# One K tile's multiply, add and score split into two halves of its keys, in a one-core decode kernel

## The chip, the core and the metric

The kernel runs on one core of a Trainium2 chip. The metric is device time in microseconds (us) of one execution. A core has five engines that run side by side: TensorE (PE; its weight loads are shown as PEld), VectorE (DVE), ScalarE (ACT), GpSimd (POOL) and SyncE (SP). Each works through its own instructions in order and waits on semaphores for the others. Sixteen DMA engines move data between the large memory (HBM) and the core's own memory; here SyncE issues nearly all of these transfers.

## The reference

One token goes through attention over a long cache (32 heads, 65,536 keys of 128 numbers each, bf16) and, beside it, through a small gated feed-forward network; a scalar gate mixes the two.

```python
def _A_ref(x, k_cache, v_cache, wq, wo):
    q = (x @ wq).reshape(B, Sq, H, Dh) -> (B, H, Sq, Dh)
    scores = einsum("bhqd,bhkd->bhqk", q, k_cache) * (Dh ** -0.5)
    p = softmax(scores)
    o = einsum("bhqk,bhkd->bhqd", p, v_cache)
    return o.reshape(B, Sq, H * Dh) @ wo

def _B_ref(x, w_gate, w_up, w_down):
    return (silu(x @ w_gate) * (x @ w_up)) @ w_down

g = sigmoid((x * gate_w).sum(-1))
return g * _A_ref(x, ...) + (1 - g) * _B_ref(x, ...)
```

K and V are 512 MB each, and every byte is read once. There are few operations per byte.

## The kernel before

**Tiles.** A head's 65,536 keys are four tiles of 128 partitions x 128 keys; tile n belongs to head n // 4. Two tiles form a pair m = n // 2, loaded by one 8.4 MB transfer (some are loaded as two tiles). K pairs alternate between two buffers (`K_bufs`), V pairs share one (`V_buf`). With one query, the scores are not made by a matrix product with K: VectorE multiplies a K tile by the query, which is repeated over the keys (`product`, L281), and then adds the upper half of the 128 columns to the lower half (`add_halves`, L293, or `add_once`, L304). TensorE adds up what is left: `scores` (L508) multiplies groups of 4 columns by a unit matrix and accumulates them in PSUM, so that 64 columns take 16 matrix products of 512 columns (128 keys x 4) each. VectorE reduces the last 4 to one score for each key (`fold`, L315). ScalarE makes the exponentials, and TensorE multiplies them with the V tiles (`values`, L531, 64 products for a pair).

**Stages.** A prologue written out by hand does the queries of all heads, the feed-forward network, and the scores of the first head (tiles 0 to 3). Then a loop goes over the pairs: in step m the scores of K pair m and the values of V pair m - 2. The change lies in the prologue.

**Order on the engines in the prologue.** After tile 2's product and addition VectorE runs the gate's operations on the feed-forward network: it waits for ScalarE's exponential `eg`, adds one, takes the reciprocal, and multiplies with the two projections (L636 to L641), which gives `hT`. TensorE uses `hT` in the product with w_down (L643, 14 matrix products, into `b_ps`); ScalarE scales that row, TensorE takes it into the output's accumulators (L651), and spreads the second head's query over the partitions (`query_spread`, L521). VectorE meanwhile multiplies tile 3 (`product(3)`), reduces tile 2, adds tile 3 (`add_halves(3)`), and TensorE makes tile 3's scores (`scores_direct(3)`). `fold(3)` and the maximum over the head's scores (`row_max`, L321) follow, and then the loop begins with tile 4.

**Transfers around the change.** SyncE issues, in its program's order: the third K pair when the scores of tile 1 are done (L629), the first V pair into `V_buf` when w_down's product is done, as w_down lies in that buffer (L654), the fourth K pair when tile 3's scores are done (event `pe_D`, L665), and in the loop the second V pair when the values of the first are done (`load_v`, L201), followed by the next K pair.

**Events.** `dv` counts VectorE's finished instructions, `pe_D` the tiles scored in the prologue, `pe_x` some of TensorE's products. `wait(engine, events, value)` holds that engine until the count is reached.

Of the kernel before, what the change touches and what calls it, by code (L numbers as in the profile page):

```python
# [8 lines left out]
ALU = mybir.AluOpType  # L9
AXIS = mybir.AxisListType  # L10
P = 128
NB = 128
PAIR = 2 * NB
QUAD = 4


WIDE = 64
# [24 lines left out]
def kernel(  # L42
# [18 lines left out]
    _, H, Sk, Dh = A_k_cache.shape  # L61
# [17 lines left out]
    def sb(name, shape, dtype=f32):  # L79
        return consts.tile(shape, dtype, name=name)  # L80
# [3 lines left out]

    K_bufs = [ring.tile([P, PAIR * Dh], bf16, name=f"K{i}_buf") for i in range(2)]
    V_buf = ring.tile([P, PAIR * Dh], bf16, name="V_buf")
# [8 lines left out]
    ident_b, ones_b, q_diag = (sb(n, [P, P], bf16) for n in ("ident_b", "ones_b", "q_diag"))  # L95
# [16 lines left out]
    S_ps = [psum.tile([P, NB, QUAD], f32, name=f"S{i}_ps") for i in range(2)]  # L112
# [14 lines left out]
    def halves(buf):  # L127
        return [buf[:, i * NB * Dh : (i + 1) * NB * Dh].rearrange("p (j d) -> p j d", d=Dh) for i in range(2)]

    K_half, V_half = [halves(b) for b in K_bufs], halves(V_buf)  # L130
# [3 lines left out]
    def v_view(n):  # L134
        return {N - 4: K_half[0][1], N - 3: V_half[0], N - 2: V_half[1], N - 1: K_half[1][1]}[n]

    sync, act, dve, pool, pe = nc.sync, nc.scalar, nc.vector, nc.gpsimd, nc.tensor
# [6 lines left out]
    ac, ac_loop, ac_q, dv, dv_loop, dv_top, dv_max, dv_first, dv_rg, out_a, out_b, pe_D, pe_K, pe_q0 = (  # L144
        Events(nc, n)
        for n in (
            "ac", "ac_loop", "ac_q", "dv", "dv_loop", "dv_top", "dv_max", "dv_first", "dv_rg",
            "out_a", "out_b", "pe_D", "pe_K", "pe_q0",
        )
    )  # L150
# [17 lines left out]
    def wait(engine, events, value):  # L168
        key = id(engine), id(events)
        value -= taken.get(key, 0)  # L170
        if seen.get(key, 0) < value:
            engine.wait_ge(events.sem, value)
            seen[key] = value
# [85 lines left out]
    marks = {}  # L259

    own = [dv]

    def product(n):
        K = K_half[n // 2 % 2][n % 2]
        q = q_sb[n // G % 2]
        q_rep = bass.AP(tensor=q.tensor, offset=q[:, :].offset, ap=[list(q[:, :].ap[0]), [0, NB], [1, Dh]])
        m = n // 2

        if m == 0:
            wait(dve, (ka_in, kb_in)[n], 16)  # L270
        elif m == 1:
            wait(dve, kc_in, 16)
        elif n == N - 1:
            wait(dve, kb_in, 32)
        else:
            wait(dve, k_in[m % 2], 16 * (m // 2))
        if n < G:
            wait(dve, ac, marks["q"])
        else:
            wait(dve, ac_q, n // G)  # L280
        return own[0](dve.tensor_tensor(out=K, in0=K, in1=q_rep, op=ALU.mult))  # L281

    def add_halves(n, width, last, out=None, ahead=None):
        K = K_half[n // 2 % 2][n % 2]
        half, mark = Dh // 2, last
        while half >= width:
            wait(dve, own[0], mark)
            to = K[:, :, 0:half]
            if half == width and ahead is not None:
                fold(ahead)  # L290
            if half == width and out is not None:
                to = out
            ins = dve.tensor_tensor(out=to, in0=K[:, :, 0:half], in1=K[:, :, half : 2 * half], op=ALU.add)  # L293
            if half == width and out is not None:
                ins.then_inc(c_S[n % 2], 1)
            else:
                mark = own[0](ins)
            half //= 2
        marks["K", n] = mark

    def add_once(n, last):
        wait(dve, own[0], last)
        K, half = K_half[n // 2 % 2][n % 2], Dh // 2
        dve.tensor_tensor(  # L304
            out=K[:, :, 0:half], in0=K[:, :, 0:half], in1=K[:, :, half:], op=ALU.add
        ).then_inc(c_S[0], 1)


    def fold(n):
        h, g = divmod(n, G)  # L310
        if n < G or n >= N - G:
            wait(dve, pe_D, n + 1 if n < G else n + 1 - N + 2 * G)
        else:
            wait(dve, pe_S, n + 1 - G)
        return own[0](dve.tensor_reduce(  # L315
            out=S_sb[h % 2][:, g * NB : (g + 1) * NB], in_=S_ps[n % 2], axis=AXIS.X, op=ALU.add
        ))
# [19 lines left out]
    def vector_step(m):  # L337
        h, b = divmod(m, MH)
        width, to = (WIDTH, T_sb) if m < M - 2 else (WIDE, None)
        last = product(2 * m)  # L340
        if to is not None:
            add_once(2 * m, last)
        if b == 0:
            top_of(h - 1)
        else:
            fold(2 * m - 1)
        if to is None:
            add_halves(2 * m, width, last)
        last = product(2 * m + 1)
        if b == 1:  # L350
            weight(h - 1, m - 1)
        add_halves(2 * m + 1, width, last, to, 2 * m)
        if b == 1:
            row_max(h, fold(2 * m + 1))
# [31 lines left out]
    def copy(out, in_, scale=1.0):  # L386
        return act.activation(out=out, in_=in_, func=ACT.Copy, scale=scale)  # L387
# [115 lines left out]
        pe.wait_ge(credit, 1)  # L503
        pe.sem_inc(credit, -1)  # L504

    def scores(n, src, width, events):
        for c in range(0, width, QUAD):
            ins = pe.matmul(  # L508
                S_ps[n % 2], lhsT=ident_b, rhs=src[:, :, c : c + QUAD],
                start=(c == 0), stop=(c == width - QUAD),  # L510
            )
            if c == 0 and events is pe_S and n == 1:
                pe_K(ins)
        events(ins)

    def scores_direct(n):
        wait(pe, dv, marks["K", n])
        scores(n, K_half[n // 2 % 2][n % 2], WIDE, pe_D)

    def query_spread(events):  # L520
        events(pe.matmul(qb, lhsT=ones_b, rhs=q_diag, start=True, stop=True))  # L521
# [34 lines left out]
    def prologue():  # L556
        with nc.allow_non_contiguous_dma(reason="small"):
# [3 lines left out]
            out=V_buf[:, : KT * H * Dh], in_=A_wq.rearrange("(p t) f -> p (t f)", t=KT)  # L561
# [17 lines left out]
        for h in range(H):  # L579
            for t in range(KT):  # L580
                ins = pe.matmul(
                    q_all[:, h : h + 1], lhsT=wq_sb[:, t, h * Dh : (h + 1) * Dh],
                    rhs=xT[:, t : t + 1], start=(t == 0), stop=(t == KT - 1),
                )
# [8 lines left out]
        marks["q"] = ac(copy(q_sb[0], qb))  # L593

        add_halves(0, WIDE, product(0))
        scores_direct(0)
        wait(dve, x_in, 16)
        wait(dve, gw_in, 16)
# [6 lines left out]
        last = product(1)  # L605
        fold(0)
        add_halves(1, WIDE, last)
        scores_direct(1)
        wait(dve, ac, marks["eg2"])
        wait(dve, dv, dv(dve.tensor_scalar_add(eg2, eg2, 1.0)))  # L610
        wait(dve, dv, dv(dve.reciprocal(gval, eg2)))
        marks["rest"] = dv(dve.tensor_scalar(
            out=rest[0:1, :], in0=gval[0:1, :], scalar1=-1.0, scalar2=1.0, op0=ALU.mult, op1=ALU.add
# [3 lines left out]
        for w in range(2):  # L617
            cols = wgu_sb[:, w].rearrange("p t (m c) -> p t c m", c=FT)
            for ft in range(FT):
                for t in range(KT):  # L620
                    ins = pe.matmul(
                        gu_ps[:, w * FT + ft : w * FT + ft + 1], lhsT=cols[:, t, ft, :],
                        rhs=xT[:, t : t + 1], start=(t == 0), stop=(t == KT - 1),
                    )
# [7 lines left out]
        last = product(2)  # L632
        fold(1)
        add_halves(2, WIDE, last)
        scores_direct(2)
        wait(dve, ac, marks["eg"])  # L636
        wait(dve, dv, dv(dve.tensor_scalar_add(eg, eg, 1.0)))
        wait(dve, dv, dv(dve.reciprocal(eg, eg)))
        wait(dve, dv, dv(dve.tensor_tensor(out=hprod, in0=gu_sb[:, :FT], in1=eg, op=ALU.mult)))
        wait(pe, wd_in, 16)  # L640
        wait(pe, dv, dv(dve.tensor_tensor(out=hT, in0=hprod, in1=gu_sb[:, FT:], op=ALU.mult)))  # L641
        for t in range(FT):
            ins = pe.matmul(  # L643
                b_ps, lhsT=hT[:, t : t + 1], rhs=wd_sb[:, t, :], start=(t == 0), stop=(t == FT - 1)
            )
        pe_x(ins)
        wait(act, dv, marks["rest"])
        wait(act, pe_x, 4)
        wait(pe, ac, ac(copy(b_sb, b_ps, rest[0:1, :])))
        for i, a in enumerate(a_ps):  # L650
            pe.matmul(  # L651
                a, lhsT=ones_f[0:1, 0:1], rhs=b_sb[:, i * HD : (i + 1) * HD], start=True, stop=False
# [5 lines left out]
        query_spread(pe_q0)  # L658
        wait(act, pe_q0, 2)
        ac_q(copy(q_sb[1], qb))  # L660
        last = product(3)
        fold(2)
        add_halves(3, WIDE, last)
        scores_direct(3)
        wait(sync, pe_D, 4)  # L665
        load_k(3)
        row_max(0, fold(3))
# [5 lines left out]
    def tensor_step(m):  # L673
        second = m % MH
        if second:
            take(c_P)
            total()
        take(c_S[0])
        scores(0, K_half[m % 2][0], WIDE, pe_S)
        if not second:  # L680
            take(c_P)
        take(c_V)
        for i in range(2):
            pe_V(values(P_sb[:, i * NB :], V_half[i], 0, NB, i == 0, i == 1))
        if not second:
            total()
        take(c_q)
        query_spread(pe_q)
        take(c_S[1])
        scores(1, T_sb, WIDTH, pe_S)  # L690
        take(c_o)
        head_turn()
        take(c_m)
        max_turn()
# [123 lines left out]
```

## Time and profile before

| what | value |
|---|---|
| median of 3 runs | 2520.32 us (2519.13 to 2520.52) |
| the profiled execution | 2520.22 us |
| its span, first to last instruction | 2518.4 us |
| PE, busy share of the span | 59% |
| DVE, busy share | 80% |
| ACT, busy share | 7% |
| main DMA queue, share of 16 engines' span | 99.8% |
| mean granted TensorE clock | 0.774 of full speed |

The profile shows one execution. A group row names line, engine, operation, output <- input, shape and count, then the busy time in us, the mean ns of one instruction, and the idle time of the engine just before, with what ended most of it. A timeline row has start and duration in us, then the same names; in brackets stands the idle time before it and its releaser. A row of the stretches' table has the stretch and its length in us, the busy time and number of instructions of PE, PEld, DVE, ACT and POOL, then the granted TensorE clock, the busy share of the DMA engines and GB/s. The ends of matrix products are modelled. Busy shares over the whole span hide which wait ends last in each stage, so the stage around the change is read by itself.

### The profile page before, as it was taken

Reading aid. Unit: us, or ns where it says so; the run is one execution under the profiler, and the core shown is the slowest. Engines: PE = TensorE matmul, PEld = TensorE weight load, DVE = VectorE, ACT = ScalarE, POOL = GpSimd, SP = SyncE. Lnnn points to the kernel's source line nnn. Section 1 sums busy time; section 2 is a strip of 40 time slices with the busy share of each in tenths; the row PEclk is TensorE's granted clock in tenths of the full one; section 3 lists DMA queues with packets and bytes.
Section 4 is the critical chain, followed back from the end, with each engine's and each line's share of the span. In section 5 each row is a group of like instructions: output and inputs, shape, how many; then the busy total and the mean of one; then the engine's idle time right before and its main releaser. Section 6 shows DMA issues by size and latency. Waiting matters only on the chain. (4 is left out here: it accounts for less than half of the span.)

```text
span 2518.4 us, 15666 instructions
## 1 busy us (share of the span) xinstructions
PE 1485.8 (59%) x6573; PEld 615.6 (24%) x6573; DVE 2003.5 (80%) x676; ACT 182.5 (7%) x503; POOL 0.7 (0%) x6
## 2 busy tenths in 40 slices
PE   2655646557556566465565564655755646557568
PEld 1322222222222222222222222222212222222223
DVE  5887877977878878779788787787887877977881
ACT  0000000000000000000000000000000000000000
POOL 0000000000000000000000000000000000000000
PEclk8777778778777787787787777877877778778789
DMA  9999999999999999999999999999999999999999
GB/s 413 424 432 432 433 433 433 434 433 434 433 433 433 433 433 435 439 438 434 433 433 434 434 433 433 433 433 433 433 435 438 438 434 434 433 434 434 433 429 388
DMA packets 22541, 1087.80 MB, mean 432 GB/s; under 512 B 2689, under 2 KB 3202, under 8 KB 4482
## 3 DMA queue, kind: packets, MB, share of 16 engines
q1 hardware_dynamic: 22242, 1087.65, 99.8%
q8 instruction: 7, 0.11, 0.0%
q10 hardware_dynamic: 288, 0.00, 0.0%
q14 instruction: 4, 0.03, 0.0%
HBM read 1087.64 MB, written 0.00 MB: 432 GB/s over the span
## 5 line engine op out<-in xcount | busy, mean ns | idle before, releaser
L281 DVE TENSOR_TENSOR K_buf<-K_buf,q_sb 128x16384 bf16<-128x16384 bf16 x128 | 1111.9, 8687 | 344.1 <-DMA K_buf<-in_A_k_cache_dram 344.1
L508 PE MATMUL S_ps<-K_buf,ident_b 128*128 128x512 bf16 x1088 | 387.2, 531 | 866.7 <-PEq L504 829.5
L531 PE MATMUL O_ps<-V_buf,P_sb 128*4 128x512 bf16 x3968 | 866.8, 379 | 31.8 <-PEq L504 31.4
L531 PEld LDWEIGHTS O_ps<-V_buf,P_sb 128*4 128x4 bf16 x3968 | 332.9, 85 | 563.3 <-issue 60.8
L293 DVE TENSOR_TENSOR K_buf<-K_buf 128x8192 bf16<-128x8192 bf16 (+1 forms) x128 | 438.2, 3423 | 3.1
L508 PEld LDWEIGHTS S_ps<-K_buf,ident_b 128*128 128x128 bf16 x1088 | 132.5, 126 | 1099.6 <-issue 1029.2
L304 DVE TENSOR_TENSOR K_buf<-K_buf 128x8192 bf16<-128x8192 bf16 x60 | 265.5, 4425 | 2.0
L387 ACT ACTIVATE O_sb<-O_ps 4x512 f32<-4x512 f32 x63 | 63.3, 1005 | 1705.2 <-PE qm_ps L521 1671.0
L315 DVE TENSOR_REDUCE S_sb<-S_ps 128x128 f32<-128x512 f32 x128 | 88.2, 689 | 110.3 <-PE S_ps L508 108.3
L524 PE MATMUL qm_ps<-diag,ones_f 128*128 128x128 f32 x126 | 34.0, 357 | 72.4 <-PEq L504 70.3
L539 PE MATMUL oh_ps<-ident_f,O_sb 4*128 4x1 f32 x504 | 64.3, 244 | 18.8 <-PEq L504 18.8
L293 DVE TENSOR_TENSOR T_sb<-K_buf 128x2048 bf16<-128x2048 bf16 x60 | 72.9, 1215 | 0.0
L539 PEld LDWEIGHTS oh_ps<-ident_f,O_sb 4*128 4x128 f32 x504 | 60.7, 186 | 48.7 <-issue 48.7
L508 PE MATMUL S_ps<-T_sb,ident_b 128*128 128x512 bf16 x240 | 64.7, 391 | 0.0
L524 PEld LDWEIGHTS qm_ps<-diag,ones_f 128*128 128x128 f32 x126 | 21.9, 218 | 76.7 <-issue 76.7
L387 ACT ACTIVATE bias<-top 128x1 f32<-128x1 f32 x32 | 6.5, 203 | 436.7 <-DVE top L325 436.7
L527 PE MATMUL tot_ps<-rs,ones_f 128*128 128x2 f32 (+1 forms) x126 | 24.5, 264 | 18.1 <-PEq L504 18.1
L387 ACT ACTIVATE oT<-whole_o,rg 32x1 f32 (+1 forms) x115 | 33.8, 294 | 4.7
L412 ACT ACTIVATE P_sb<-S_sb,bias 128x256 bf16<-128x256 f32 x62 | 31.5, 508 | 1.0
L527 PEld LDWEIGHTS tot_ps<-rs,ones_f 128*128 128x128 f32 x126 | 20.1, 200 | 36.9 <-issue 36.9
L334 DVE RECIPROCAL recip<-tot_ps 128x1 f32<-128x1 f32 x1 | 0.2, 169 | 32.0 <-PE tot_ps L527 32.0
L508 PEld LDWEIGHTS S_ps<-T_sb,ident_b 128*128 128x128 bf16 x240 | 20.7, 96 | 15.9
(61 smaller groups left out, 214.5 us busy)
## 6 DMA issues: line engine op xcount, KB each, us to landing
K_buf<-in_A_k_cache_dram SPq DMA_DIRECT2D x4, 4096.0 KB, 32.9
V_buf<-in_A_v_cache_dram SPq DMA_DIRECT2D x2, 4096.0 KB, 21.6
V_buf<-in_A_v_cache_dram SPq DMA_DIRECT2D x4, 2048.0 KB, 23.1
V_buf<-in_A_wq_dram SPq DMA_DIRECT2D x1, 4096.0 KB, 12.3
K_buf<-in_A_v_cache_dram SPq DMA_DIRECT2D x1, 4096.0 KB, 34.7
K_buf<-in_A_v_cache_dram SPq DMA_DIRECT2D x3, 1024.0 KB, 28.3
K_buf<-in_A_wo_dram SPq DMA_DIRECT2D x1, 2048.0 KB, 25.5
V_buf<-in_B_w_gate_dram SPq DMA_DIRECT2D x1, 1792.0 KB, 54.5
```

The lines of the kernel that those rows point to most:

```text
L281: return own[0](dve.tensor_tensor(out=K, in0=K, in1=q_rep, op=ALU.mult))
L293: ins = dve.tensor_tensor(out=to, in0=K[:, :, 0:half], in1=K[:, :, half : 2 * half], op=ALU.add)
L304: dve.tensor_tensor(out=K[:, :, 0:half], in0=K[:, :, 0:half], in1=K[:, :, half:], op=ALU.add).then_inc(c_S[0], 1)
L315: return own[0](dve.tensor_reduce(out=S_sb[h % 2][:, g * NB : (g + 1) * NB], in_=S_ps[n % 2], axis=AXIS.X, op=ALU.add))
L334: wait(dve, own[0], own[0](dve.reciprocal(recip[:, 0:1], total)))
L387: return act.activation(out=out, in_=in_, func=ACT.Copy, scale=scale)
L412: return act.activation(out=out, in_=S_sb[h % 2][:, b * PAIR : b * PAIR + count], func=ACT.Exp, bias=bias[:, 0:1], scale=scale, accum_out= ...
L508: ins = pe.matmul(S_ps[n % 2], lhsT=ident_b, rhs=src[:, :, c : c + QUAD], start=(c == 0), stop=(c == width - QUAD),)
L524: pe.matmul(mT, lhsT=ones_f, rhs=diag, start=True, stop=True).then_inc(pe_m.sem, n)
L527: pe_t(pe.matmul(tot[:, :n], lhsT=ones_f, rhs=rs[:, :n], start=True, stop=True))
L531: ins = pe.matmul(O_ps, lhsT=probs[:, j : j + 4], rhs=view[:, j : j + 4, :], start=(opens and j == start), stop=(closes and j == stop - 4),)
L539: ins = pe.matmul(oh, lhsT=O_sb[:, c * Dh : (c + 1) * Dh], rhs=ident_f[0:4, c : c + 1], start=(opens and c == 0), stop=(c == 3),)
```

## The change

Tile 3's product, its addition and its scores are each done in two halves of the tile's 128 keys. `product`, `scores` and `scores_direct` take a range of keys, and a new function `add_some` adds the column halves for a range. VectorE's order becomes: first half's product, the gate's operations, first half's addition, second half's product, the reduction of tile 2, second half's addition. TensorE's order becomes: w_down's product, the scores of the first half (16 products of 256 columns), the accumulators' row and the query's spread as before, the scores of the second half (16 products of 256 columns). The event `pe_D` is raised only by the second half. All else keeps its place.

```diff
-    def product(n):
-        K = K_half[n // 2 % 2][n % 2]
+    def product(n, start=0, stop=NB):
+        K = K_half[n // 2 % 2][n % 2][:, start:stop, :]
         q = q_sb[n // G % 2]
-        q_rep = bass.AP(tensor=q.tensor, offset=q[:, :].offset, ap=[list(q[:, :].ap[0]), [0, NB], [1, Dh]])
+        q_rep = bass.AP(tensor=q.tensor, offset=q[:, :].offset, ap=[list(q[:, :].ap[0]), [0, stop - start], [1, Dh]])
...
+    def add_some(n, last, start, stop):
+        wait(dve, own[0], last)
+        K, half = K_half[n // 2 % 2][n % 2][:, start:stop, :], Dh // 2
+        marks["K", n] = own[0](dve.tensor_tensor(
+            out=K[:, :, 0:half], in0=K[:, :, 0:half], in1=K[:, :, half:], op=ALU.add
+        ))
...
-    def scores(n, src, width, events):
+    def scores(n, src, width, events, start=0, stop=NB):
         for c in range(0, width, QUAD):
             ins = pe.matmul(
-                S_ps[n % 2], lhsT=ident_b, rhs=src[:, :, c : c + QUAD],
+                S_ps[n % 2][:, start:stop, :], lhsT=ident_b, rhs=src[:, start:stop, c : c + QUAD],
                 start=(c == 0), stop=(c == width - QUAD),
             )
...
-        events(ins)
-
-    def scores_direct(n):
+        if stop == NB:
+            events(ins)
+
+    def scores_direct(n, start=0, stop=NB):
         wait(pe, dv, marks["K", n])
-        scores(n, K_half[n // 2 % 2][n % 2], WIDE, pe_D)
+        scores(n, K_half[n // 2 % 2][n % 2], WIDE, pe_D, start, stop)
...
         scores_direct(2)
+
+        first_half = product(3, 0, NB // 2)
         wait(dve, ac, marks["eg"])
...
         wait(pe, dv, dv(dve.tensor_tensor(out=hT, in0=hprod, in1=gu_sb[:, FT:], op=ALU.mult)))
+        add_some(3, first_half, 0, NB // 2)
         for t in range(FT):
             ins = pe.matmul(
                 b_ps, lhsT=hT[:, t : t + 1], rhs=wd_sb[:, t, :], start=(t == 0), stop=(t == FT - 1)
             )
         pe_x(ins)
+        scores_direct(3, 0, NB // 2)
...
-        last = product(3)
+        last = product(3, NB // 2, NB)
         fold(2)
-        add_halves(3, WIDE, last)
-        scores_direct(3)
+        add_some(3, last, NB // 2, NB)
+        scores_direct(3, NB // 2, NB)
```

## The prediction

> **What bounds the kernel now.** The first view is the profile's page: its HBM line and the costliest group of instructions.
>
> ```profile
> HBM read 1087.64 MB, written 0.00 MB: 432 GB/s over the span
> ...
> L281 DVE TENSOR_TENSOR K_buf<-K_buf,q_sb 128x16384 bf16<-128x16384 bf16 x128 | 1111.9, 8687 | 344.1 <-DMA K_buf<-in_A_k_cache_dram 344.1
> ```
>
> VectorE's largest group waits 344 us in total for K tiles to land; the page names no other releaser for that group. So the next view is the table of busy time by stretch, whose last two columns are the busy share of the DMA engines and what they moved: the 100 us in which the change and its consequences lie, the long stretch after them, and four slices of the first.
>
> ```profile
> 64.00:164.00 100.00, 66.37 (x322) 28.43 (x321) 81.37 (x31) 7.96 (x22) 0.00 (x0) 0.77 0.98 421
> ...
> 164.00:2364.00 2200.00, 1289.79 (x5519) 528.82 (x5520) 1794.38 (x596) 163.14 (x449) 0.00 (x0) 0.76 1.00 434
> ...
> 121.00:122.00 1.00, 1.00 (x7) 0.36 (x5) 0.27 (x1) 0.00 (x0) 0.00 (x0) 1.00 0.45 197
> 122.00:123.00 1.00, 1.00 (x6) 0.40 (x5) 0.00 (x0) 0.00 (x0) 0.00 (x0) 1.00 0.01 0
> 123.00:124.00 1.00, 1.00 (x8) 0.48 (x6) 0.00 (x0) 0.00 (x0) 0.00 (x0) 1.00 0.00 0
> 124.00:125.00 1.00, 0.96 (x5) 0.19 (x2) 0.79 (x1) 0.92 (x1) 0.00 (x0) 1.00 2.38 786
> ```
>
> From 164 us on the transfers run at share 1.00 and 434 GB/s. Between 121 and 124 us they run dry (a packet is booked where it starts, so the last ones still finish in this gap). At 434 GB/s the 1087.64 MB alone take 2506 us, so of the 2518.4 us span only some 12 us are start, end and this hole. An earlier VectorE or TensorE is worth something only if it closes the hole.
>
> Third view, SyncE's DMA issues in order of time (start, duration), then the list of issues, asked one by one: the last number is us from issue to landing.
>
> ```profile
> 57.79 0.33 SPq L182 DMA_DIRECT2D K_buf<-in_A_k_cache_dram  x1
> 78.06 0.33 SPq L182 DMA_DIRECT2D V_buf<-in_A_v_cache_dram  x1
> 89.36 0.33 SPq L182 DMA_DIRECT2D K_buf<-in_A_k_cache_dram  x1
> 123.68 0.33 SPq L182 DMA_DIRECT2D V_buf<-in_A_v_cache_dram  x1
> 124.30 0.33 SPq L182 DMA_DIRECT2D K_buf<-in_A_k_cache_dram  x1
> 159.49 0.33 SPq L182 DMA_DIRECT2D V_buf<-in_A_v_cache_dram  x1
> ...
> 199.37 0.33 SPq L182 DMA_DIRECT2D V_buf<-in_A_v_cache_dram  x1
> ```
>
> ```profile
> K_buf<-in_A_k_cache_dram SPq DMA_DIRECT2D x1, 27.7
> ...
> V_buf<-in_A_v_cache_dram SPq DMA_DIRECT2D x1, 26.7
> ...
> K_buf<-in_A_k_cache_dram SPq DMA_DIRECT2D x1, 34.8
> ...
> V_buf<-in_A_v_cache_dram SPq DMA_DIRECT2D x1, 21.6
> K_buf<-in_A_k_cache_dram SPq DMA_DIRECT2D x1, 41.6
> ...
> V_buf<-in_A_v_cache_dram SPq DMA_DIRECT2D x1, 25.7
> ...
> V_buf<-in_A_v_cache_dram SPq DMA_DIRECT2D x1, 24.4
> ```
>
> Call the pairs K2, V0, K3, V1, K4, V2 and V3 in the order of the two lists (K5, issued just after V2, is left out). Issue plus landing time gives 85.5, 104.8, 124.2, 145.3, 165.9, 185.2 and 223.8. V2 to V3 is two pairs in 38.6 us, 19.3 each; V0 to K3 takes 19.4; but K3 to V1 takes 21.1 and V1 to K4 20.6. **The hole costs 1.8 + 1.3 = 3.1 us.** The 100 us at 421 instead of 434 GB/s say the same: 100 x (1 - 421/434) = 3.0. V1 was issued 0.5 us ahead of K3's landing and lost 3.1, so a lead of 0.5 + 3.1 = 3.6 us is enough; V3 has 24.4 - 19.3 = 5.1 and loses nothing.
>
> V1's issue waits for the 64 products of the first V pair (L531), these for scores of tile 4, these for VectorE's product of tile 4, and that stands in VectorE's queue behind tile 3, which the change splits.
>
> **The change part by part.** VectorE's timeline around it, and the one row that prices half an addition:
>
> ```profile
> 62.37 4.42 DVE L293 TENSOR_TENSOR K_buf<-K_buf 128x8192 bf16<-128x8192 bf16 x1
> 69.12 0.18 DVE L637 TENSOR_SCALAR eg<-eg 128x14 f32<-128x14 f32 x1 [2.33 <-ACT eg L628]
> ...
> 69.91 8.69 DVE L281 TENSOR_TENSOR K_buf<-K_buf,q_sb 128x16384 bf16<-128x16384 bf16 x1
> 78.51 0.68 DVE L315 TENSOR_REDUCE S_sb<-S_ps 128x128 f32<-128x512 f32 x1
> 79.11 4.42 DVE L293 TENSOR_TENSOR K_buf<-K_buf 128x8192 bf16<-128x8192 bf16 x1
> 89.36 0.69 DVE L315 TENSOR_REDUCE S_sb<-S_ps 128x128 f32<-128x512 f32 x1 [5.84 <-PE S_ps L508]
> ...
> 90.69 8.68 DVE L281 TENSOR_TENSOR K_buf<-K_buf,q_sb 128x16384 bf16<-128x16384 bf16 x1
> ```
>
> ```profile
> L293 DVE TENSOR_TENSOR K_buf<-K_buf 128x4096 bf16<-128x4096 bf16 x1 | 2.3, 2291 | 0.0
> ```
>
> *VectorE.* Before, it stands idle 2.33 us for the gate's exponential. After, the first half product of tile 3 fills that wait. A half product has 8192 elements, as the 4.42 us addition has, so two halves cost 2 x 4.42 - 8.69 = 0.15 us more; two half additions 2 x 2.29 - 4.42 = 0.16 more. New order: half product 66.8 to 71.2, gate operations (69.91 - 69.12 = 0.8) to 72.0, half addition to 74.3, half product to 78.7, the reduction of tile 2 (0.6) to 79.3, half addition to 81.6. It ended at 83.5: 2.0 earlier, which is 2.33 - 0.31 within the rounding. The exponential is in at 69.1, before the half product ends, so the moved wait holds nothing; the added ones are on VectorE's own last product, as before.
>
> *TensorE*, with two late rows as prices at the full granted clock, and one stretch of the clock (third number from the right):
>
> ```profile
> 68.47 6.45 PE L508 MATMUL S_ps<-K_buf,ident_b 128*128 128x512 bf16 x16
> 74.85 3.18 PE L643 MATMUL O_ps<-V_buf,hT 128*1 128x512 bf16 x14
> 78.87 1.02 PE L651 MATMUL a_ps<-O_sb,ones_f 1*1 1x256 f32 x4 [0.83 <-ACT O_sb L387]
> ...
> 83.58 5.74 PE L508 MATMUL S_ps<-K_buf,ident_b 128*128 128x512 bf16 x16 [3.54 <-DVE K_buf L293]
> ...
> 103.98 5.77 PE L508 MATMUL S_ps<-K_buf,ident_b 128*128 128x512 bf16 x16 [12.16 <-PEq L504]
> 109.68 13.97 PE L531 MATMUL O_ps<-V_buf,P_sb 128*4 128x512 bf16 x64
> ...
> 2434.03 3.64 PE L508 MATMUL S_ps<-K_buf,ident_b 128*128 128x512 bf16 x16 [0.26 <-DVE K_buf L293]
> ...
> 2474.80 1.91 PE L548 MATMUL a_ps<-K_buf,oT 128*1 128x256 bf16 x16
> ```
>
> ```profile
> 77.80:81.30 3.50, 1.41 (x7) 0.33 (x5) 3.50 (x3) 1.25 (x3) 0.00 (x0) 0.97 1.25 543
> ```
>
> hT is 2 us later (72.0), but TensorE reaches w_down's product only at 74.85, after the scores of tile 2: hidden with 2.9 us to spare, and without that cover it would cost 2 us. w_down's end, and with it V0's issue (78.06), stays. No row shows 16 score products of 256 columns. Below: the 1.91 us of L548's 16 with 256 columns. Above: no saving at all from halving, 6.45. I take 1.9 at the full clock and twice that, 3.8, at half, since the 512-column row (3.64 at full, 6.45 mostly at half) nearly scales so and L548 is the nearest shape. The first half's 16 run from 78.0 to 79.9, or 81.8 at worst, and delay L651 and the query's spread by 1 to 3 us; the copied query is needed only by tile 4's product at 85.5, which hides it. The first half's new wait is for an addition done at 74.3 and so holds nothing. The second half's does hold TensorE, but behind it stand only the turn of the maxima and tile 4's scores, which need VectorE's later work anyway. It starts at 81.6 and ends at 83.5 to 85.4 (before: 89.3).
>
> The Trainium skill (TensorE: Matmul & The Clock Gate, Part 1: The HAM clock gate) says that the array returns to half clock after an idle window of about 3.4 us. By that rule the extra scores in the stretch after 77.8 keep the clock up, since TensorE's busy time there rises from 1.41 us to some 3.3, and the second half costs 1.9; without it 3.8.
>
> *What follows.* The reduction and the maximum (90.69 - 89.36 = 1.3) end at 84.8 to 86.7; tile 4's product cannot start before K2 lands at 85.5. So it starts at 85.5 to 86.7 instead of 90.69, 4.0 to 5.2 earlier. The V products then start at 104.5 to 105.7 by that shift, but not before V0's landing at 104.8. If tile 4's scores, now 5.77 us, ran wholly at half clock, they would take at most 2 x 3.64 = 7.3, 1.5 more: 104.8 to 107.2. V1 is issued 14.0 after their start (123.68 - 109.68), at 118.8 to 121.2: a lead over K3's landing of 3.0 to 5.4, where 3.6 suffices. K3's issue moves up from 89.36 to about 84.5, but the transfers have K2 and V0 before it, so it lands at 124.2 as now.
>
> **Sum.** DMA hole -3.1 (at the shortest lead, 0.6 under what suffices, -2.5); VectorE +0.3 and TensorE's second set of 16 are inside the shift, not on the path. Nothing is given back: V2's issue waits for V1 (3.1 earlier) and for K3's scores (unchanged), so it comes 0 to 3.1 earlier than 159.5; K4's new landing is 165.9 - 3.1 = 162.8, and even at 159.5 the lead is 3.3, at most 0.3 short of what suffices. Span 2518.4 - 3.1 = 2515.3. The profiled execution took 2520.22, 1.8 more than its span, and the median is 2520.32; I forecast 2520.3 - 3.0 = **2517.3**.
>
> The Trainium skill (DMA: Bandwidth & Descriptors, Where 436 GB/s comes from) puts the fabric's ceiling at 435 GB/s. This trace agrees with 434. By it nothing beyond the hole can be won here.
>
> **The rivals.**
> - *Nothing comes through* (0.10): a wait takes the place of the one removed, K2's or V0's landing later than read, or V1 is early and the transfers thin out in the same place. For it: both landings are within 1 us of when they are needed. Against: the bounds above already contain them. 2520.3.
> - *Halves as dear as wholes* (0.05): 256 columns cost 6.45, so the second half ends at 88.1, tile 4's product starts at 89.4, V1 comes 1.3 earlier: 2519.0. Against: L548.
> - *Slower, by the granted clock* (0.03): the shorter scores leave TensorE at half clock when the V products begin. These 64 then take up to 28 us (twice 13.97), and V1 comes 14 - 4.5 = 9.5 later: 2530. It decides if the clock is still half after the scores of tile 4. Against: those 16 products are unchanged and raised the clock before.
> - *Faster by more than the hole* (0.02): a higher transfer rate would be needed; 1% of it is 25 us: 2495. No row speaks for it.
>
> **How the numbers follow.** The forecast has 0.80, with its own range 2516.1 to 2518.5 (2.5 to 3.5 gained, and 0.7 either way, half of the 1.4 between the runs shown). The range 2516.0 to 2520.2 adds the halves-as-dear case and the lower part of the first rival. What a measurement can tell from no change is about 0.2%, 5 us: forecast and first two rivals lie inside it, 0.93 with a little taken off for mechanisms not thought of; slower 0.04, faster 0.03.
>
> **What would show it.** Right: transfers at 434 GB/s through 121 to 125 us, V1 issued near 119, K4 landing near 162.8, and tile 4's product waiting for K2 or starting by 86.7. Wrong: V1 issued after 121.5, a hole elsewhere before 200 us, or more than 5 us of difference.

## The result, and the profile after

The changed kernel takes 2516.64 us (median of 22 runs, 2516.29 to 2517.2), the kernel before 2520.23 us (22 runs, 2518.9 to 2521.85). The ratio is 0.9985, with a 95% interval of 0.9979 to 0.9991: 3.6 us faster. The profiled executions differ by 3.35 us, 2520.22 to 2516.87, and their spans by 3.3, 2518.4 to 2515.1.

The table of busy time by stretch, of the changed kernel (columns as before: the last two are the busy share of the DMA engines and GB/s):

```profile
64.00:164.00 100.00, 64.26 (x341) 29.80 (x340) 82.59 (x34) 7.92 (x22) 0.00 (x0) 0.77 1.01 435
121.00:122.00 1.00, 0.80 (x6) 0.74 (x6) 0.00 (x0) 0.52 (x3) 0.00 (x0) 0.88 1.14 459
122.00:123.00 1.00, 0.86 (x4) 0.51 (x3) 0.00 (x0) 0.47 (x3) 0.00 (x0) 0.50 1.42 590
123.00:124.00 1.00, 0.00 (x0) 0.00 (x0) 0.00 (x0) 0.00 (x0) 0.00 (x0) 0.50 0.46 197
124.00:125.00 1.00, 0.00 (x0) 0.00 (x0) 0.96 (x1) 0.00 (x0) 0.00 (x0) 0.50 1.66 721
```

The hole is gone: 459 and 590 GB/s start in the slices that read 197 and 0 (a packet is booked where it starts, so single slices jump), and the 100 us run at 435 instead of 421. TensorE and VectorE now stand idle at 123 us, and it costs nothing.

SyncE's issues in the changed kernel, then us from issue to landing of the last five, V0, K3, V1, K4 and V2:

```profile
57.69 0.33 SPq L182 DMA_DIRECT2D K_buf<-in_A_k_cache_dram  x1
77.96 0.33 SPq L182 DMA_DIRECT2D V_buf<-in_A_v_cache_dram  x1
83.30 0.33 SPq L182 DMA_DIRECT2D K_buf<-in_A_k_cache_dram  x1
118.83 0.33 SPq L182 DMA_DIRECT2D V_buf<-in_A_v_cache_dram  x1
119.44 0.33 SPq L182 DMA_DIRECT2D K_buf<-in_A_k_cache_dram  x1
157.52 0.33 SPq L182 DMA_DIRECT2D V_buf<-in_A_v_cache_dram  x1
```

```profile
V_buf<-in_A_v_cache_dram SPq DMA_DIRECT2D x1, 26.7
...
K_buf<-in_A_k_cache_dram SPq DMA_DIRECT2D x1, 40.7
...
V_buf<-in_A_v_cache_dram SPq DMA_DIRECT2D x1, 24.5
...
K_buf<-in_A_k_cache_dram SPq DMA_DIRECT2D x1, 43.5
...
V_buf<-in_A_v_cache_dram SPq DMA_DIRECT2D x1, 24.7
```

K3 lands at 124.0, as before (124.2), though it was issued 6.1 us earlier. V1 is issued 5.2 us ahead of that landing instead of 0.5. It lands at 143.3, K4 at 162.9, V2 at 182.2: 19.3, 19.6 and 19.3 us apart, where they had been 21.1, 20.6 and 19.3.

VectorE and TensorE in the changed kernel, and the granted clock (third number from the right) in two stretches:

```profile
66.76 4.42 DVE L281 TENSOR_TENSOR K_buf<-K_buf,q_sb 128x8192 bf16<-128x8192 bf16 x1
71.10 0.17 DVE L647 TENSOR_SCALAR eg<-eg 128x14 f32<-128x14 f32 x1
...
71.87 2.29 DVE L304 TENSOR_TENSOR K_buf<-K_buf 128x4096 bf16<-128x4096 bf16 x1
74.07 4.42 DVE L281 TENSOR_TENSOR K_buf<-K_buf,q_sb 128x8192 bf16<-128x8192 bf16 x1
78.41 0.68 DVE L322 TENSOR_REDUCE S_sb<-S_ps 128x128 f32<-128x512 f32 x1
79.01 2.28 DVE L304 TENSOR_TENSOR K_buf<-K_buf 128x4096 bf16<-128x4096 bf16 x1
83.31 0.69 DVE L322 TENSOR_REDUCE S_sb<-S_ps 128x128 f32<-128x512 f32 x1 [2.02 <-PE S_ps L515]
...
85.37 8.69 DVE L281 TENSOR_TENSOR K_buf<-K_buf,q_sb 128x16384 bf16<-128x16384 bf16 x1 [0.65 <-DMA K_buf<-in_A_k_cache_dram]
```

```profile
74.75 3.18 PE L654 MATMUL O_ps<-V_buf,hT 128*1 128x512 bf16 x14
77.87 1.93 PE L515 MATMUL S_ps<-K_buf,ident_b 128*128 128x256 bf16 x16
...
81.34 1.93 PE L515 MATMUL S_ps<-K_buf,ident_b 128*128 128x256 bf16 x16 [0.44 <-DVE K_buf L304]
...
98.66 4.90 PE L515 MATMUL S_ps<-K_buf,ident_b 128*128 128x512 bf16 x16 [12.90 <-PEq L511]
104.82 13.97 PE L539 MATMUL O_ps<-V_buf,P_sb 128*4 128x512 bf16 x64 [1.26 <-PEq L511]
```

```profile
77.80:81.30 3.50, 3.10 (x22) 1.79 (x21) 3.49 (x3) 1.25 (x3) 0.00 (x0) 1.00 1.25 543
81.40:84.70 3.30, 1.87 (x16) 1.39 (x16) 1.36 (x2) 0.00 (x0) 0.00 (x0) 1.00 0.78 338
```

Tile 4's product now waits 0.65 us for K2 to land, in place of VectorE's own queue. The V products start at 104.82, just after V0 lands at 77.96 + 26.7 = 104.7. By these two waits more earliness of tile 3 would be worth nothing here.

### The profile page after: what moved, and what is told of

It is laid out like the page before. It is cut to its first block, busy times and chain, and to the rows that moved or that the text cites. A ratio compares the mean times of both kernels' runs of the same rounds, so it can differ in the third digit from the quotient of the medians.

```text
span 2515.1 us, 15700 instructions
## 1 busy us (share of the span) xinstructions
PE 1483.7 (59%) x6589; PEld 616.1 (24%) x6589; DVE 2003.5 (80%) x678; ACT 182.3 (7%) x503; POOL 0.7 (0%) x6
## 5 line engine op out<-in xcount | busy, mean ns | idle before, releaser
L281 DVE TENSOR_TENSOR K_buf<-K_buf,q_sb 128x16384 bf16<-128x16384 bf16 (+1 forms) x129 | 1112.0, 8620 | 348.9 <-DMA K_buf<-in_A_k_cache_dram 348.9
L515 PE MATMUL S_ps<-K_buf,ident_b 128*128 128x512 bf16 (+1 forms) x1104 | 385.2, 523 | 867.5 <-PEq L511 834.5
L293 DVE TENSOR_TENSOR K_buf<-K_buf 128x4096 bf16<-128x4096 bf16 (+1 forms) x127 | 433.7, 3415 | 3.1
L535 PEld LDWEIGHTS tot_ps<-rs,ones_f 128*128 128x128 f32 x126 | 20.1, 201 | 36.6 <-issue 36.6
```

The costliest lines, as they stand in the source:

```text
L515: ins = pe.matmul(S_ps[n % 2][:, start:stop, :], lhsT=ident_b, rhs=src[:, start:stop, c : c + QUAD], start=(c == 0), stop=(c == width - QUAD),
L535: pe_t(pe.matmul(tot[:, :n], lhsT=ones_f, rhs=rs[:, :n], start=True, stop=True))
```

## The experiments

The question was what the 3.6 us hang on: V1's lead over K3's landing (the theory), the earliness of tile 3's work as such, K3's earlier issue, or one of the two halves of the change. The table gathers all ten kernels tried, with the two of the change, by V1's lead. The lead (K3's issue plus its landing time, minus V1's issue), K4's landing and the next column are from the one profiled execution; the median is over all runs of that kernel. The profiled execution was the slowest of 11 runs with the scores whole and the fastest of 11 with the halves after the gate, so a lead goes with the time of its own execution first. In the run with K3 very late the hole lies one transfer earlier, so K3's own lead over V0's landing stands there. The kernel before, measured again beside each group, had medians from 2519.91 to 2520.63, so differences of a few tenths between rows mean nothing.

| kernel | K3 issue + landing | V1 issue | lead | K4 lands | profiled us | median us | lowest to highest |
|---|---|---|---|---|---|---|---|
| changed kernel | 83.30 + 40.7 | 118.83 | 5.2 | 162.9 | 2516.87 | 2516.64 | 2516.29 to 2517.2 |
| K3 late | 94.79 + 29.6 | 119.26 | 5.1 | 163.1 | 2516.69 | 2516.78 | 2516.29 to 2517.31 |
| whole product first | 84.98 + 39.2 | 119.43 | 4.7 | 162.9 | 2517.21 | 2517.21 | 2516.34 to 2519.69 |
| V products late, 60 copies | 83.59 + 40.5 | 119.50 | 4.6 | 162.9 | 2517.59 | 2517.83 | 2516.48 to 2520.31 |
| whole product first, then halves | 84.63 + 39.5 | 119.65 | 4.5 | 163.6 | 2517.98 | 2516.96 | 2516.39 to 2518.98 |
| halves after the gate | 87.08 + 37.1 | 121.52 | 2.7 | 164.1 | 2518.30 | 2519.34 | 2518.3 to 2521.46 |
| scores whole | 87.77 + 36.6 | 122.36 | 2.0 | 166.2 | 2521.07 | 2518.96 | 2517.4 to 2521.07 |
| V products late, 66 copies | 83.47 + 40.8 | 122.90 | 1.4 | 165.5 | 2520.05 | 2519.82 | 2519.09 to 2522.57 |
| K3 very late (K3 for V0) | 77.36 + 27.5 (V0) | 103.97 (K3) | 0.9 | 165.6 | 2519.61 | 2520.54 | 2519.51 to 2521.7 |
| kernel before | 89.36 + 34.8 | 123.68 | 0.5 | 165.9 | 2520.22 | 2520.23 | 2518.9 to 2521.85 |
| V products late, 73 copies | 84.49 + 39.4 | 127.20 | -3.3 | 169.9 | 2523.92 | 2522.50 | 2521.34 to 2523.96 |
| V products late, 90 copies | 85.11 + 39.1 | 131.85 | -7.6 | 174.4 | 2528.23 | 2527.99 | 2526.89 to 2528.29 |

Read so, the prediction's rule (lost is what a lead under 3.6 us lacks) can be tested in each execution, by how much later than the changed kernel's 162.9 K4 lands. In eight of the ten kernels tried it comes out within 0.4 us: 1.2 us late at a lead of 2.7 (the rule gives 0.9), 2.6 at 1.4 (2.2), 11.5 at -7.6 (11.2), nothing lost at 4.6 and 4.7. At 4.5 K4 is 0.7 late where the rule gives nothing, and at 2.0 it is 3.3 late where the rule gives 1.6. The delay is not made good later: each profiled execution ends within 1.0 us of it.

**V products late.** The idle copies stand on ScalarE between the first head's maxima and its exponentials.

```diff
         max_turn(2)
+        for _ in range(60):
+            idle = ac(copy(idle_sb, ident_f[:, :96]))
+            wait(act, ac, idle)
```

> The changed kernel, with 60 idle copies on ScalarE between the first head's maxima and its first exponentials, so that only the first V products, and with them V1's issue, come late; tile 3's work stays as early as in the changed kernel. At an estimated 0.37 us a copy the exponentials are done at about 108.3 us instead of 99.6, the V products start there instead of at 104.8, V1 is issued near 122.3. Theory (only V1's lead over K3's landing at 124.0 counts, 3.6 suffices): lead 1.7, a hole of 1.9 us is back, 2518.5 us. Rival (the time follows how early tile 3 is scored and VectorE's wait is filled): tile 3 is as early as before this edit, so 2516.6 us. Rival (everything on the chain is worth its own length): 2516.6 + 3.5 = 2520.1 us.

A copy takes 0.314 us, not 0.37 (60 of them 18.84), so V1 came only 0.7 us later than in the changed kernel. The profiled execution (2517.59 us) shows no hole: K4 lands at 162.9 at a lead of 4.6. Yet the median is 2517.83 and runs reach 2520.31; what lead those runs had, and whether they lost their time at this place, is not on record. As a test of the theory this dose was too small, so it was raised.

> The first run with 66 idle copies instead of 60 (0.314 us a copy by that run's trace): exponentials done at 106.8, V1 issued at about 121.4, lead over K3's landing 2.8 us. Theory in its first form (what a lead under 3.6 lacks is lost): 0.8 us, 2517.4 us. Second form (as soon as some DMA engines run dry, nearly the whole 3 us are lost): 2519 to 2520 us. Rival (earliness of tile 3's scores pays by itself): 2516.6 us.

> 73 idle copies: V1 issued at about 123.6, where the kernel before issues it, lead 0.5 us, with tile 3's scores as early as in the changed kernel. Theory in both forms: 3.1 us lost and the changed kernel's whole gain with them, 2519.7 to 2520.2 us. Rival (earliness of tile 3's scores pays by itself): 2516.6 us.

> 90 idle copies: V1 issued at about 128.9, 4.7 us after K3's landing. Theory in its first form: 3.6 + 4.7 = 8.3 us lost, 2525 us, slower than the kernel before although tile 3 is scored 6 us earlier. Second form: 3.1 + 5 to 3.1 + 4.7 us, 2524 to 2525 us. Rival (a hole is made good later because the loop has slack): 2520 us or less.

The three rows that say most, from SyncE's issues, TensorE's timeline and the stretches of the run with 73 copies:

```profile
127.20 0.33 SPq L183 DMA_DIRECT2D V_buf<-in_A_v_cache_dram  x1
```

```profile
110.51 16.66 PE L540 MATMUL O_ps<-V_buf,P_sb 128*4 128x512 bf16 x64 [6.20 <-PEq L512]
```

```profile
125.00:126.00 1.00, 1.00 (x7) 0.41 (x5) 1.00 (x1) 0.00 (x0) 0.00 (x0) 1.00 0.00 0
```

V1 came 3.6 us later than meant: after the 6.20 us pause the 64 products took 16.66 us instead of 13.97, and the maxima came about a microsecond later too. So these runs are read by the lead that they had. At -3.3 and -7.6 the first form of the theory (lost is what a lead under 3.6 lacks) gives 6.9 and 11.2 us; lost were 7.1 and 11.4 in the executions that had these leads, 5.9 and 11.4 by the medians. At 1.4 it gives 2.2 and 3.2 were lost. Between leads of 0.5 and 2.7 the two forms are not told apart: K4's delay of 1.2 us at 2.7 fits the first, its 3.3 at 2.0 the second. The rival that tile 3's earliness pays by itself falls: with 90 copies tile 3 is scored 4 us earlier than before the change (K3, issued when its scores are done, at 85.11 instead of 89.36), and it takes 7.4 us more than the kernel before measured beside it (2527.99 to 2520.63; ratio 1.0029, interval 1.0019 to 1.004).

**K3 late.** The issue of K3 is moved behind 30 such copies; then behind 60.

```diff
-        wait(sync, pe_D, 4)
-        load_k(3)
...
         max_turn(2)
+        for _ in range(30):
+            idle = ac(copy(idle_sb, ident_f[:, :96]))
+            wait(act, ac, idle)
+        wait(sync, pe_D, 4)
+        wait(sync, ac, idle)
+        load_k(3)
```

> The changed kernel, with 30 idle copies on ScalarE after the first head's maxima, and K3's issue held until they are done: issue at about 96.3 us instead of 83.3, later than the 89.4 of the kernel before; the V products keep their place (exponentials done at about 97.2, before they are needed). Theory: K3 stands behind K2 and V0 in the transfers, V0 lands at 104.7, a lead of 8.4 us is more than the 3.6 that suffice, so nothing changes: 2516.6 us. Rival (part of the gain is K3's issue, 6.1 us earlier than before): 13 us later costs some of the gain or all of it, 2518 to 2520.2 us.

> K3's issue held behind 60 idle copies, at about 104.2 us, 0.8 us ahead of V0's landing (105.0) where 30 copies left it 10 us ahead; V1 still issued at about 119.5. Theory: the same hole opens one transfer earlier, K3 lands near 127 instead of 124.2, about 2.8 to 3.1 us lost, 2519.5 to 2519.9 us, with V1's lead over K3's landing at 7. Rival (only V1's place matters): 2516.6 to 2517.8 us.

The issue of K3 in the first of the two, and us to its landing:

```profile
94.79 0.33 SPq L183 DMA_DIRECT2D K_buf<-in_A_k_cache_dram  x1
```

```profile
K_buf<-in_A_k_cache_dram SPq DMA_DIRECT2D x1, 29.6
```

Issued 11.5 us later than in the changed kernel, K3 lands at 124.4 instead of 124.0, and the time is 2516.78 us: K3's earlier issue is no part of the gain. Issued 0.9 us ahead of V0's landing, it costs 3.9 us by the medians (2.7 by the spans, 2517.8 to 2515.1), though V1 is issued at 119.20. What pays is a lead at each transfer, not V1's place.

**One part of the change at a time.** VectorE in the changed order, tile 3's scores whole:

```diff
         pe_x(ins)
-        scores_direct(3, 0, NB // 2)
...
-        scores_direct(3, NB // 2, NB)
+        scores_direct(3)
```

> VectorE in the changed order and in halves, but tile 3's scores whole, 16 products of 512 columns after the second half's addition. Scores from 81.3 to 85.0 (clock up) or 87.1 (half clock), tile 4's product at 86.3 to 88.4, V1 issued at 119.8 to 121.9 against K3's landing at 124.0. Theory: lead 2.1 to 4.2, so 0 to 1.5 us of the 3.6 us gain is lost: 2516.6 to 2518.1 us, and by the lead that the profile shows. Rival (the time follows how early tile 4 begins): 0.9 to 3.0 of 5.3 us of earliness are gone, 2517.2 to 2518.7 us. Rival (the split scores are what pays): 2520.2 us.

The halves alone, with VectorE in the order of before:

```diff
-        first_half = product(3, 0, NB // 2)
...
-        add_some(3, first_half, 0, NB // 2)
...
-        scores_direct(3, 0, NB // 2)
...
-        last = product(3, NB // 2, NB)
+        last = product(3)
         fold(2)
+        add_some(3, last, 0, NB // 2)
+        scores_direct(3, 0, NB // 2)
```

> The other part alone: VectorE keeps the order of before (gate's operations, then tile 3's whole product), only the addition and the scores are in halves. First half's addition ends at 81.3, its scores start there after TensorE has been idle for 1.3 us, so at half clock: 3.5 us, to 84.8; second half's scores 1.9 to 3.5 us, to 86.7 to 88.3; tile 4's product at 88.1 to 89.6, V1 at 121.2 to 123, lead 1.2 to 3. Theory: 1.5 to 3 us of the 3.6 us gain are lost, 2518 to 2519.6 us. Rival (halving the scores is the gain): 2516.6 us. Rival (filling VectorE's wait is the gain): 2520.2 us.

The first missed the theory's range: V1 came at 122.36, later than the latest time expected, and the median is 2518.96 instead of 2518.1 at most; by its own lead of 2.0 the rule gives 2518.2. Against the medians of the kernel before measured beside them (2520.31 and 2519.91), the parts alone save 1.3 us and 0.6 us, where both together save 3.6; their ratios, 0.9994 (interval 0.9985 to 1.0003) and 0.9998 (0.9989 to 1.0007), do not exclude that either saves nothing. V1's lead grows by 1.5 and by 2.2 us, and by 4.7 with both.

**The whole product ahead of the gate**, one line of the kernel before moved and nothing split, and then the same with addition and scores in halves:

```diff
         scores_direct(2)
+        last = product(3)
         wait(dve, ac, marks["eg"])
...
-        last = product(3)
         fold(2)
```

> The kernel before with one line moved and nothing split: tile 3's whole product stands ahead of the gate's operations. hT at 76.3, so w_down's product starts 1.5 us later (76.3), V0 is issued at 79.5, its lead over K2's landing (85.4) stays 5.9. Addition ends at 81.3, scores whole to 85.0 or 87.1, tile 4's product at 86.3 to 88.4, V1 at 119.8 to 121.9. Theory: 2516.6 to 2518.1 us, as with VectorE in halves and the scores whole. Rival (w_down's later product or V0's later issue is on the path): 1.5 us more, 2518 to 2519.6 us. Rival (the halves are what pays): 2520.2 us.

> Tile 3's whole product ahead of the gate's operations as in the fourth run, but addition and scores in halves as in the changed kernel. w_down's product at 76.3 to 79.5, first half's scores to 81.4, second half's to 83.4 at the full clock, tile 4's product waits for K2 at 85.4, V1 at 118.8 to 119.5 in every run. Theory: 2516.6 us, all runs within 1 us, where the whole scores spread over 3.4 us. Rival (the spread came from w_down's and V0's later place): 2517.2 us, runs up to 2519.5 again.

Both come within 0.6 us of the changed kernel by their medians (ratios to the kernel before 0.9990, interval 0.9981 to 0.9999, and 0.9988, interval 0.9979 to 0.9997), but runs reach 2519.69 and 2518.98, and the halves did not narrow that: the expectation of runs within 1 us fell. Moving one line, with nothing split, thus brings most of the gain, 3.1 us against the kernel before measured beside it. Both have leads of 4.5 to 4.7. Why filling VectorE's wait gives a lead of 2.0 with half products and 4.7 with the whole one is seen in TensorE's rows and clock. First the run with half products and whole scores, then the run with the whole product:

```profile
81.50 6.25 PE L515 MATMUL S_ps<-K_buf,ident_b 128*128 128x512 bf16 x16 [1.87 <-DVE K_buf L304]
```

```profile
77.80:81.30 3.50, 1.18 (x5) 0.33 (x5) 3.50 (x3) 1.16 (x3) 0.00 (x0) 0.81 1.12 487
81.40:84.70 3.30, 3.20 (x8) 1.16 (x9) 0.04 (x1) 0.00 (x0) 0.00 (x0) 0.50 0.83 357
```

```profile
76.29 3.18 PE L644 MATMUL O_ps<-V_buf,hT 128*1 128x512 bf16 x14 [1.73 <-DVE hT L642]
...
81.33 3.63 PE L508 MATMUL S_ps<-K_buf,ident_b 128*128 128x512 bf16 x16
```

```profile
77.80:81.30 3.50, 2.67 (x13) 0.79 (x12) 3.28 (x1) 0.97 (x2) 0.00 (x0) 1.00 1.21 524
81.40:84.70 3.30, 3.30 (x17) 1.36 (x15) 0.00 (x0) 0.28 (x1) 0.00 (x0) 1.00 0.74 318
```

The same 16 products start within 0.2 us of each other and take 6.25 us at a clock of 0.50 or 3.63 at 1.00. TensorE was busy for 1.18 of the 3.5 us before them in the one, and for 2.67 in the other, where w_down's product had come 1.9 us later (76.29 instead of 74.43). The kernel before agrees: busy for 1.41 of those 3.5 us, it took 5.74 us for the 16 products; so do the halves after the gate, busy for 1.18, with a clock of 0.66 from 81.4 to 84.7. That the work in the stretch before decides the clock is thus argued from these kernels; no run changed that work alone.

By the medians none of these kernels beats the changed one.

## Why the prediction was right, point by point

- *The transfers bound the kernel, and the change is worth the hole.* Right. The 100 us run at 435 GB/s, and the kernels fall into order by a transfer's lead, not by VectorE's or TensorE's place. Where two rows stand the wrong way round, it is by 0.9 us at most, between medians whose leads come from one execution each.
- *VectorE.* Right: the half product starts at 66.76, the half additions take 2.29 and 2.28, and the last ends at 81.3 (81.6 forecast). The gate's exponential held nothing.
- *TensorE.* Right at the lower end: 1.93 us for 16 products of 256 columns, at the full clock, both times, so halves as dear as wholes are out. The first half's scores fill the stretch after 77.8 (busy 3.10 us, 3.3 forecast), and the clock stayed at 1.00. That this filling keeps the clock up was argued there by the Trainium skill (TensorE: Matmul & The Clock Gate, Part 1: The HAM clock gate); the run with whole scores agrees as to the clock, 0.50 after a stretch with 1.18 us of work, though that stretch was not idle.
- *K2's landing as the next wait.* Right: tile 4's product waits for it and starts at 85.37 (forecast: 85.5 at the earliest). V1 is issued at 118.83 (118.8 to 121.2), K4 lands at 162.9 (162.8).
- *"A lead of 3.6 us is enough".* Right for most of the profiled executions, but weakly founded: it was read off one point, the kernel before, as if each microsecond of lead saved a microsecond. At leads of 4.6 and 4.7 K4 lands as in the changed kernel; at 2.0 it lands 3.3 us late where the rule gives 1.6. V1's own lead came out at 5.2, so the doubt did not matter. The rule also says nothing of how the runs of one kernel differ: with 4.5 to 4.7 in the profiled execution the medians lose 0.3 to 1.2 us and single runs up to 3.7, and only the two kernels with 5.1 and 5.2 kept all their runs below 2517.4 us. Why is open, as each kernel has one trace.
- *The size.* 3.0 us forecast; 3.6 measured by the medians, just above the 2.5 to 3.5 given for the gain, and 3.35 between the profiled executions. The median came out at 2516.64 instead of 2517.3. The hole itself was sized right: K4 lands 3.0 us earlier, at 162.9 where 162.8 was forecast. The spans differ by 0.3 more than that, and the changed kernel's median lies 0.2 below its profiled execution; no term of the sum stands for either. The runs of the kernel before scatter over 3.0 us, not the 1.4 of the three shown, and those of the changed kernel over 0.9. What a measurement can tell was put too coarsely at 5 us: the interval of the ratio is a gain of 2.3 to 5.3 us.
- *The slower rival.* It did not come true in this change. In the runs with idle copies its mechanism showed, smaller than priced: 16.66 us for the V products after a pause, where 28 had been put as the most.

## What to carry to other kernels

In a kernel that the transfers bound, look for the stretches in which they run dry, price the change by these alone, and follow back what issues the late transfer; work saved elsewhere on the engines is not in the sum. A straight line through one bad point gave the loss within 0.4 us in eight of ten executions here; to keep all runs fast, take the lead from the steady part of the trace (5.1 us here, which lost nothing). When work is split or moved on TensorE, look at how busy the stretch ahead of it leaves the engine: here the same products took 6.25 us or 3.63.

## What the runs showed of the hardware

After the queue has run dry, the first packets of a transfer start 0.9 to 1.0 us after its issue. In the kernel before, where V1 is issued at 123.68, the stretches up to 124.60 and 124.70 show it; with 73 and 90 copies packets start again between 0.9 and 1.0 us after the issue too.

```profile
123.70:124.60 0.90, 0.90 (x7) 0.47 (x7) 0.39 (x1) 0.52 (x1) 0.00 (x0) 1.00 0.00 0
124.60:124.70 0.10, 0.10 (x2) 0.00 (x0) 0.10 (x1) 0.10 (x1) 0.00 (x0) 1.00 10.07 3277
```

A transfer does not land all at once. The trace has 16 landing events for each of these transfers, and the landing times used here are the last of them. K3's in the kernel before come at 122.3 to 122.6 (13 of them) and at 123.8 to 124.2 (three). For V1's packets to start no later than K3's first event, V1 would have to be issued about 1.9 + 1.0 = 2.9 us ahead of the last one. This estimate covers most of the 3.6 us. In the run with scores whole 15 of V1's events come at 143.6 to 144.2 and one at 146.6, and its loss is larger than the rule's; why that one is late stays open.

A transfer issued 11.5 us later landed at nearly the same time (124.4 and 124.0), because the ones before it were still running: in that run it was issued at 94.79 and V0 landed at 105.1.
